# Attention with routed experts: rows of pages and of h turned by DMA transposes instead of TensorE

## The chip, the cores and the metric

The kernel runs on one core of a Trainium2 chip. The metric is the device time of one execution in microseconds, lower is better. Three runs of the kernel before gave 420.01, 420.77 and 420.65 us, median 420.65. The profile was taken in an execution of its own, which took 408.61 us.

## What is computed

The reference is block-causal attention over 8 sequences with 8 heads, 576 positions and head width 64, followed by a layer of 8 experts, of which each of the 4608 tokens uses one.

```python
scores = scale * np.matmul(q, k.transpose(0, 1, 3, 2))
mask = (pos[:, None] // 64) >= (pos[None, :] // 64)
attn = softmax(np.where(mask, scores, -1e9))          # written out in the reference
x = np.matmul(attn, v).transpose(0, 2, 1, 3).reshape(4608, 512)
logits = x @ w_gate                                   # 512 -> 8
expert_idx = np.argmax(logits, axis=1)
gate_w = softmax(logits)[np.arange(N), expert_idx]
for e in range(8):                                    # the rows of expert e
    h = np.maximum(x_sorted[lo:hi] @ w1[e], 0.0)      # 512 -> 1024
    y_sorted[lo:hi] = h @ w2[e]                       # 1024 -> 512
out = gate_w[:, None] * y
```

The softmax lines stand for the reference's own longer form; the rest is cut from it.

## The kernel before

**Attention.** The 64 (batch, head) slices are taken as 32 pairs of two heads; four pairs make one batch. The loop at L595 is a software pipeline written out by hand: the order of the instructions on TensorE, ScalarE and GpSimd is the order of the code, while VectorE's and SyncE's are placed by the compiler's priorities. In the turn of pair p, SyncE issues the loads of pair p+3 (q and k) and p+2 (v), GpSimd casts q and k of p+2 to f16 (`cast`, L202 and L204), TensorE computes the scores of p+1, the attention product of p (`attend`, L276), and the transposes of q and k of p+2 (`trans`, L212). `sums` adds the exponentials over key blocks on VectorE (L251, L257, L259). `denominators` (L282) then collects, in one PSUM tile, the softmax denominators (lhsT `picks`) and the router's logits (lhsT `wg`) as rows; VectorE copies it to `dl` (L305). `finish(p-1)` (L307) transposes the output of the pair before (L319, L322) and its `dl`, takes the reciprocals, and writes the scaled rows as f16 into `x16` and the scaled logits into `lgp`.

**Routing.** `choose` (L355) sums the logits of a batch and makes the one-hot choice `oh`. `route` (L376) counts with six small matmuls (L381, L385) how many earlier tokens of the batch chose the same expert. `places` (L392) turns the ranks into slots. `scatter` (L441, L447) sends the rows of the batch, 258 words each (512 f16 values in 256 words, then the gate weight and the number of the token), from GpSimd to the DRAM tile `xsorted`. That tile is made of pages of 128 rows, and each page belongs to one expert. The first ten pages are those known to be closed before the last two batches (`order1`); the others are listed in `order2`, which is written in the expert stage.

**Weights.** `load_weights(n)` (L125) is one of 32 DMAs on GpSimd's queue that read f32 and write f16 into `wall`. A partition p holds rows that lie next to each other in the matrix: `(p a b) f`. One such DMA is issued in each pair from the fourth on, two in each of the last three.

**Experts.** Each page is a tile T. `mload(T)` (L674) loads its 128 rows of 258 words with one SyncE DMA; the page's number comes from a register that SyncE loads from `order1` or `order2` (L670). `mtx` (L684) transposes the 512 columns in four TensorE transposes into PSUM, taking every fourth column to suit the weights' layout, and VectorE copies them to `xsT` (L691). `m1` (L698) is the first product, eight matmuls of 512 columns; ScalarE applies the relu (L708). `mth` (L711) transposes h in eight TensorE transposes, every eighth column, and VectorE copies (L718). `m2` (L721) is the second product, eight matmuls; ScalarE scales by the gate weight (L728) and GpSimd scatters the rows to the output by their token numbers (L729). `step(T)` (L737) issues m1(T), mtx(T+1), mth(T-1), m2(T-2), and loads page T+5. The last batch's finish and choice are in step 0, its ranks and scatters in step 1, `order2` in step 3. In this run 38 pages are in use.

In this stage only TensorE and ScalarE follow the code's order; SyncE does nothing but load pages, from ten buffers.

Of the kernel before, what the change touches and what calls it, by code (L numbers as in the profile page):

```python
# [10 lines left out]
I32 = mybir.dt.int32  # L11
# [11 lines left out]
def kernel(  # L23
# [33 lines left out]
    picks = consts.tile([128, 2, 32], F32)  # L57
    wg = consts.tile([128, HP, 32], F32)
    ione = consts.tile([128, E], F32)
# [22 lines left out]
    def gate_weights():  # L82
        nc.vector.memset(wg, 0.0)
        nc.vector.memset(picks, 0.0)
        for h in range(2):
            nc.vector.memset(picks[:, h, h:h + 1], 1.0)
        gate = moe_w_gate.rearrange("(hp h d) e -> h d hp e", h=2, d=64)
        for h in range(2):
            nc.sync.dma_start(out=wg[h * 64:h * 64 + 64, :, 8 + h * E:8 + h * E + E],
                              in_=gate[h])  # L90

# [33 lines left out]
    def load_weights(n):  # L125
        part, e, a = n // (2 * E), n // 2 % E, n % 2
        src = (moe_w1, moe_w2)[part][e].rearrange("(p a b) f -> p a (b f)", a=2, b=(2, 4)[part])
        nc.gpsimd.dma_start(
            out=wall[:, e, 8 * part + 4 * a:8 * part + 4 * a + 4, :].rearrange("p b f -> p (b f)"),
            in_=src[:, a, :])  # L130

    with tc.tile_pool(name="ld", bufs=2) as ld, \
# [14 lines left out]
        dls = [op.tile([128, 256], F32, name=f"dl{i}") for i in range(2)]  # L147
# [10 lines left out]
        def borders():  # L158
# [6 lines left out]
            for t in dls:  # L165
                nc.gpsimd.memset(t[:, 192:256], 1.0)
# [115 lines left out]
        def denominators(p):  # L282
# [5 lines left out]
            def add(t, cols, lhsT, src, start=False):  # L288
                nc.tensor.matmul(out=ps[32 * t:32 * t + 32, cols], lhsT=lhsT, rhs=src,  # L289
                                 start=start, stop=True, skip_group_check=True)  # L290
            lo, hi = slice(0, 128), slice(128, 192)
            for h in range(2):
                for j in range(4):
                    add(j, lo, picks[:, h, :],
                        acc[:, h, j * 128 - 128:j * 128] if j else pt[:, h, 0:128], h == 0)
            for h in range(2):
                add(h, hi, picks[:, h, :], acc[:, h, 384:448])
            for h in range(2):
                add(h, hi, picks[:, h, :], p4[:, h, :])
            for j in range(4):  # L300
                add(j, lo, wg[:, hp, :], oT[:, j * 128:j * 128 + 128])
            for t in (2, 3):
                add(t, hi, wg[:, hp, :], oT[:, 512:576])
            with tc.high_priority():
                st["dl"] = nc.vector.tensor_copy(dl[:, 0:192], ps)  # L305

        def finish(p, held=None):  # L307
# [3 lines left out]
            if hp == 0:  # L311
# [3 lines left out]
                st["lg", b] = op.tile([128, 5, H, E], F32, name="lgp")  # L315
# [5 lines left out]
            for n, src in enumerate((oT[:, 512:640], dl[:, 0:128], dl[:, 128:256])):  # L321
# [3 lines left out]
            nc.vector.reciprocal(rec[:, 4, :], ps2[:, 256:290:33])  # L325
            x16 = st["x16", b].bitcast(F16)
            for j, n, rows, logits in ((0, 4, ps, by_j[:, :, 8:24]),
                                       (4, 1, ps2[:, 0:128], ps2[:, 328:344].unsqueeze(1))):
                r = rec[:, j:j + n, :].unsqueeze(3)
                nc.vector.tensor_tensor(  # L330
                    out=x16[:, j:j + n, hp * 128:hp * 128 + 128].rearrange(
                        "p i (h d) -> p i h d", h=2),
                    in0=rows.rearrange("p (i h d) -> p i h d", h=2, d=64),
                    in1=r.to_broadcast([128, n, 2, 64]), op=ALU.mult)
                nc.vector.tensor_tensor(
                    out=st["lg", b][:, j:j + n, 2 * hp:2 * hp + 2, :],
                    in0=logits.rearrange("p i (h e) -> p i h e", h=2),
                    in1=r.to_broadcast([128, n, 2, E]), op=ALU.mult)

        def psum_small(i=1):  # L340
            return yps[i] if yps else t_ps.tile([128, 512], F32, name="tp")
# [13 lines left out]
        def choose(b):  # L355
            lg = rp.tile([128, 5, E], F32, name="lg")
            nc.vector.reduce_sum(out=lg, in_=st.pop(("lg", b)).rearrange("p j h e -> p j e h"),
# [18 lines left out]
        def route(b):  # L376
# [3 lines left out]
            rk_ps = psum_small()[:, 0:6 * E]  # L380
# [3 lines left out]
            for s in range(1, 6):  # L384
                nc.tensor.matmul(out=rk_ps[:, s * E:6 * E], lhsT=ones16,  # L385
                                 rhs=oh[:, 0:6 - s, :].rearrange("p j e -> p (j e)"),
                                 start=False, stop=(s == 5), skip_group_check=True)
            rk = rp.tile([128, 6, E], F32, name="rk")
            nc.scalar.copy(rk.rearrange("p j e -> p (j e)"), rk_ps)
# [166 lines left out]
        def last_order():  # L556
# [3 lines left out]
            ps = psum_small(0)[0:1, 0:2 * n]  # L560
# [6 lines left out]
        with tc.manual_schedule(engines={ET.PE, ET.Activation, ET.Pool}):  # L567
# [27 lines left out]
            for p in range(PAIRS):  # L595
# [12 lines left out]
                if p > HP and p % HP == 2:  # L608
                    places(p // HP - 1)
# [8 lines left out]
                if p > 2:  # L618
                    first = p - 3 + max(0, p - PAIRS + 3)
                    for n in range(first, first + 1 + (p >= PAIRS - 3)):  # L620
# [10 lines left out]
                if p > HP and p % HP == 1:  # L631
                    route(p // HP - 1)
                if p == PAIRS - 5:
                    first_places()
                if p == PAIRS - 4:
                    orders()
                denominators(p)
# [6 lines left out]
                if p >= HP and p % HP == 0:  # L644
                    with tc.high_priority():
                        choose(p // HP - 1)
                if p == PAIRS - 6:
# [6 lines left out]
            for e in range(E):  # L654
# [6 lines left out]
        xps = o_ps.tile([128, 512], F16, name="o0")  # L661
        hTps = o_ps.tile([128, F], F16, name="o1")
        xTs, hs, hTs, ys = ([m_sb.tile([128, w], dt, name=f"{n}{i}") for i in range(2)]
                            for n, w, dt in (("xsT", 512, F16), ("h16", F, F16), ("hT", F, F16),
                                             ("y", Dm, F32)))
# [8 lines left out]
        def mload(T):  # L674
            xs = xsp.tile([128, ROW], I32, name="xs")
            page = number(T, 0, ET.SP, NP - 1)
            ins = nc.sync.dma_start(
                out=xs, in_=xs_pages[:, ds(page, 1), :].rearrange("p a r -> p (a r)"))
# [143 lines left out]
```

## Time and profile before

| What | Value |
|---|---|
| median of three runs | 420.65 us |
| the profiled execution's own time | 408.61 us |
| its span, first to last instruction | 406.8 us |
| TensorE busy | 377.9 us, 93% |
| VectorE / ScalarE / GpSimd busy | 220.0 / 231.2 / 204.0 us |
| end of attention on TensorE | about 231.5 us |
| first product of tile 0, of tile 37 | 235.58 us, 391.12 us |
| end of the last second product | about 399.2 us |
| issue of the last scatter | 401.79 us |

A page of the profile gives the busy time of each engine, the span cut in 40 slices of 10.2 us with the busy share of each engine in tenths, the DMA queues, the chain of work that ended last, and the costliest groups of instructions. A line of a group or of the timeline names the engine, the line of the code, the operation, and the tiles it writes and reads. Matmuls overlap, so their durations can't be added: the distance from one start to the next is what counts. In lists of waits the columns are the waiting engine and line, what it waited for, the sum in us, the number of times and the longest. PE is TensorE, PEld its weight loads, DVE VectorE, ACT ScalarE, POOL GpSimd and SP SyncE; SPq is SyncE's queue of instructions, with the ones that issue DMAs.

### The profile page before, as it was taken

The numbers are of one execution on the slowest core, as the hardware profiler recorded it, in microseconds if no ns is written. First come the engines' busy times: TensorE is split into PE (matmuls) and PEld (weight loads), VectorE is DVE, ScalarE is ACT, GpSimd is POOL, SyncE is SP. The second block draws the span as 40 slices with busy tenths as digits, with TensorE's granted clock in tenths as the row PEclk, the third lists the DMA queues.
The fourth block names the chain that finished last, engine by engine and source line by source line (L and its number), as shares of the span: only waits on it lengthen the run. The fifth ranks groups of instructions, "written<-read, shape, count | busy, mean of one in ns | idle before, by whom it ended". The sixth has DMA issues, their size and how long they took to land.

```text
span 406.8 us, 11668 instructions
## 1 busy us (share of the span) xinstructions
PE 377.9 (93%) x4122; PEld 241.4 (59%) x4122; DVE 220.0 (54%) x683; ACT 231.2 (57%) x409; POOL 204.0 (50%) x430
## 2 busy tenths in 40 slices
PE   7899999899899899998998789999999999999992
PEld 6666667567576666675675555555555555555550
DVE  2546685886878876958978655222323222232320
ACT  4877767678677778676677223434444443434441
POOL 3666548569569477586494766412222121212222
PEclk9999999999999999999999989999999999999997
DMA  6798989999999999989998991332322222222212
GB/s 168 219 238 218 235 192 200 227 231 224 232 230 203 245 223 217 237 194 250 225 198 163 198 220 65 126 104 91 106 78 92 80 97 99 92 104 79 96 67 79
DMA packets 83068, 67.58 MB, mean 166 GB/s; under 512 B 52079, under 2 KB 75375, under 8 KB 83008
## 3 DMA queue, kind: packets, MB, share of 16 engines
q0 software_dynamic: 9824, 31.31, 33.9%
q1 hardware_dynamic: 72352, 34.89, 32.6%
q8 instruction: 37, 0.61, 0.6%
q10 hardware_dynamic: 832, 0.59, 0.5%
q14 instruction: 23, 0.19, 0.1%
HBM read 67.56 MB, written 17.23 MB: 208 GB/s over the span
## 4 chain that ended last, share of the span: by engine, by line
issue 26%; PE 25%; DMA 16%; POOL 16%; DVE 12%; ACT 2%; POOLq 1%; SPq 0%; ACTq 0%; DVEq 0%
PE o L276 9%; POOL out_dram L729 8%; PE tp L289 5%; DMA out_dram<-y,xs 4%; PE s L242 3%; DMA tl<-in_k_dram 3%; POOL xsorted L447 3%; POOL qk L202 2%; DMA qk<-in_k_dram 2%; PE o L212 2%; PE tp L319 2%; DMA xs<-xsorted 2%; POOL qk L204 2%; DMA xsorted<-x,slot 2%; PE tp L322 2%
## 5 line engine op out<-in xcount | busy, mean ns | idle before, releaser
L245 ACT ACTIVATE pt<-s 128x1024 f32<-128x1024 f32 x96 | 94.9, 1025 | 28.4 <-ACT qkT L217 10.9
L729 POOL DMA_INDIRECT out_dram<-y,xs x38 | 37.4, 984 | 110.8 <-ACT y L728 107.9
L276 PE MATMUL o<-pt,v 128*64 128x320 f32 (+3 forms) x768 | 90.0, 383 | 0.0
L703 PE MATMUL s<-wall,xsT 128*128 x304 | 73.1, 384 | 1.6 <-DVE xsT L691 1.1
L725 PE MATMUL tp<-wall,hT 128*128 x304 | 71.6, 379 | 0.0
L276 PEld LDWEIGHTS o<-pt,v 128*64 128x64 f32 x768 | 50.1, 137 | 35.4 <-issue 5.9
L691 DVE COPY xsT<-o 128x512 f16<-128x512 f16 x38 | 16.1, 423 | 100.9 <-PE o L687 100.9
L708 ACT ACTIVATE h<-s 128x1024 f16<-128x1024 f32 x38 | 38.9, 1023 | 50.3 <-PE s L703 50.3
L728 ACT ACTIVATE y<-tp,xs 128x512 f32<-128x512 f32 x38 | 26.1, 687 | 53.6 <-PE tp L725 53.6
L703 PEld LDWEIGHTS <-xsT 128*128 128x128 f16 x304 | 30.1, 99 | 37.9 <-issue 2.2
L447 POOL DMA_INDIRECT xsorted<-x,slot x40 | 43.4, 1085 | 10.1 <-issue 7.4
L247 POOL MEMSET pt<- 64x128 f32 x128 | 22.8, 200 | 46.2 <-ACT pt L245 34.8
L202 POOL CAST qk<-qk 128x512 f16<-128x512 f32 x62 | 41.1, 690 | 9.5 <-DMA qk<-in_q_dram 6.8
L725 PEld LDWEIGHTS <-hT 128*128 128x128 f16 x304 | 28.4, 98 | 27.1
L280 ACT COPY oT<-o 128x256 f32<-128x256 f32 x64 | 25.8, 403 | 29.3 <-PE o L276 29.3
L215 ACT COPY qkT<-o 128x512 f16<-128x512 f16 x62 | 36.9, 595 | 2.8 <-PE o L212 2.1
L251 DVE TENSOR_TENSOR acc<-pt 128x896 f32<-128x896 f32 x32 | 35.7, 1116 | 2.3 <-POOL pt L247 2.2
L305 DVE COPY dl<-tp 128x192 f32<-128x192 f32 x32 | 11.4, 355 | 47.1 <-PE tp L289 47.0
L257 DVE TENSOR_TENSOR acc<-acc,pt 128x640 f32<-128x640 f32 x32 | 35.2, 1099 | 0.1
L242 PE MATMUL s<-qkT 64*128 64x512 f16 (+4 forms) x320 | 32.0, 295 | 2.4 <-ACT qkT L215 1.3
L330 DVE TENSOR_TENSOR x<-tp,rec 128x512 f16<-128x512 f32 x64 | 31.1, 486 | 0.1
L718 DVE COPY hT<-o 128x1024 f16<-128x1024 f16 x38 | 26.3, 691 | 7.2 <-PE o L715 4.8
(153 smaller groups left out, 553.9 us busy)
## 6 DMA issues: line engine op xcount, KB each, us to landing
wall<-in_moe_w_dram POOLq DMA_DIRECT2D x32, 512.0 KB, 7.6
qk<-in_q_dram SPq DMA_DIRECT2D x32, 256.0 KB
v<-in_v_dram SPq DMA_DIRECT2D x64, 128.0 KB
qk<-in_k_dram SPq DMA_DIRECT2D x30, 256.0 KB
xs<-xsorted SPq DMA_DIRECT2D x43, 129.0 KB
xsorted<-fill SPq DMA_DIRECT2D x1, 1419.0 KB
tl<-in_q_dram SPq DMA_DIRECT2D x32, 32.0 KB
v<-in_v_dram SPq DMA_DIRECT2D x32, 32.0 KB
```

What stands on the lines that cost most here:

```text
L202: eng.tensor_copy(h16[:, n, 0:4].rearrange("p c h d -> p h c d"), qk[:, n].rearrange("p h (c d) -> p h c d", c=4))
L215: copy(qkT[:, n, 0:512].rearrange("d (p c) -> d p c", c=4), ps[:, 0:512].rearrange("d (c p) -> d p c", c=4))
L242: nc.tensor.matmul(out=sp[:, h, o:o + w], lhsT=qkT[r, 1, c * 128:c * 128 + 128], rhs=qkT[r, 0, q0:q0 + w], start=True, stop=True)
L245: nc.scalar.activation(pt[:, :, t * 512:t * 512 + 512], sp, AF.Exp, scale=scale)
L251: ins = nc.vector.tensor_tensor(out=acc[:, :, 0:448], in0=pt[:, :, 128:576], in1=pt[:, :, 576:1024], op=ALU.add)
L257: nc.vector.tensor_tensor(out=acc[:, :, 128:448], in0=acc[:, :, 128:448], in1=pt[:, :, 1024:1344], op=ALU.add)
L276: nc.tensor.matmul(out=o[h * 64:h * 64 + 64, q0 - lo:hi - lo], lhsT=vt[:, c, h, :], rhs=src, start=(c == 0), stop=(c == last), skip_group_ ...
L447: ins = nc.gpsimd.indirect_dma_start(out=xsorted[:, :], out_offset=bass.IndirectOffsetOnAxis(ap=slot[0:m, j:j + 1], axis=0), in_=x16[0:m, ...
L703: nc.tensor.matmul(out=hp[:, half * 512:half * 512 + 512], lhsT=xT[:, c * 128:c * 128 + 128], rhs=weight(T, 2 * c + half), start=(c == 0), ...
L708: nc.scalar.activation(h, hp, AF.Relu)
L725: nc.tensor.matmul(out=yp, lhsT=hT[:, f * 128:f * 128 + 128], rhs=weight(T, 8 + f), start=(f == 0), stop=(f == 7))
L729: ins = nc.gpsimd.indirect_dma_start(out=out[:, :], out_offset=bass.IndirectOffsetOnAxis(ap=xs[:, 257:258], axis=0), in_=y, in_offset=None ...
```

## The change

1. **Pages and h by DMA.** `mload` becomes two DMAs on SyncE: a DMA transpose of the page's 512 f16 columns straight into `xT`, and a small load of the last two words of each row, `gt`. `mtx` goes; the register of the page's expert is loaded by `expert(T)`. `mth` becomes one DMA transpose on SyncE from h into one of three `hT` buffers. It stands right behind m1(T). SyncE is now in the code's order too.
2. **Weights with rows 128 c + p.** The DMA transposes put column 128 c + p on partition p, so the weights' rows are loaded in that order: `(a b p) f`. A partition's share of one DMA is no longer one run but two (w1) or four (w2).
3. **Denominators' tile.** The last 64 positions' denominators and logits move into free rows of the same 128 columns, by lhsT `ones3` shifted and a second copy of the gate weights, `wg4`. So `dl` has 128 columns for 192 and `finish` transposes it once instead of twice.
4. **Ranks in the same tile.** `route` is split: `ranks` writes its six matmuls into columns 128 to 175 of the denominators' tile, behind them; `ranks_out` copies them on VectorE instead of ScalarE.
5. **Order.** `places` moves behind `finish`; `first_places` and `orders` go one pair later; weight loads 26 to 29 move up to pairs 28 and 29, none is left in pair 30 and two in pair 31. In the expert stage the last batch's ranks go from step 1 to 2, `last_order` from 3 to 4.

```diff
@@ gate_weights, load_weights @@
+            nc.sync.dma_start(out=wg4[h * 64:h * 64 + 64, :, h, 24:32], in_=gate[h])
...
-        src = (moe_w1, moe_w2)[part][e].rearrange("(p a b) f -> p a (b f)", a=2, b=(2, 4)[part])
+        b = (2, 4)[part]
+        src = (moe_w1, moe_w2)[part][e].rearrange("(a b p) f -> p a b f", a=2, b=b)
@@ denominators @@
             for h in range(2):
-                add(h, hi, picks[:, h, :], acc[:, h, 384:448])
+                add(h, 64, ones_at(2 + h), acc[:, h, 384:448])
...
-            for t in (2, 3):
-                add(t, hi, wg[:, hp, :], oT[:, 512:576])
+            for h in range(2):
+                add(2 + h, 64, wg4[:, hp, h, :], oT[:, 512:576])
+            if b is not None:
+                ranks(b, ps[:, 128:128 + 6 * E])
             with tc.high_priority():
-                st["dl"] = nc.vector.tensor_copy(dl[:, 0:192], ps)
+                st["dl"] = nc.vector.tensor_copy(dl, ps[:, 0:128])
+                if b is not None:
+                    ranks_out(b)
@@ finish @@
-            for n, src in enumerate((oT[:, 512:640], dl[:, 0:128], dl[:, 128:256])):
+            for n, src in enumerate((oT[:, 512:640], dl)):
@@ ranks_out, was in route @@
-            nc.scalar.copy(rk.rearrange("p j e -> p (j e)"), rk_ps)
+            nc.vector.tensor_copy(rk.rearrange("p j e -> p (j e)"), rk_ps)
@@ the loop over pairs @@
-                    first = p - 3 + max(0, p - PAIRS + 3)
-                    for n in range(first, first + 1 + (p >= PAIRS - 3)):
+                    until = {PAIRS - 4: 4 * E - 5, PAIRS - 3: 4 * E - 2, PAIRS - 2: 4 * E - 2,
+                             PAIRS - 1: 4 * E}
+                    for n in range(until.get(p - 1, p - 3), until.get(p, p - 2)):
                         load_weights(n)
...
-                denominators(p)
+                denominators(p, p // HP - 1 if p > HP and p % HP == 1 else None)
@@ mload, was one load of all 258 words @@
+            xT = xsp.tile([128, 4, 128], F16, name="xT")
+            gt = xsp.tile([128, 2], I32, name="gt")
             page = number(T, 0, ET.SP, NP - 1)
+            rows = xs_pages[:, ds(page, 1), :].rearrange("p a r -> p (a r)")
+            for ins in (nc.sync.dma_start_transpose(out=xT, in_=rows.bitcast(F16)[:, 0:512]),
+                        nc.sync.dma_start(out=gt, in_=rows[:, 256:258])):
@@ mth @@
-            for f in range(8):
-                nc.tensor.transpose(ps[:, f * 128:f * 128 + 128],
-                                    h[:, f:F:8], ident16)
-            hT = hTs[T % 2]
-            nc.vector.tensor_copy(hT, ps)
+            hT = hTs[T % 3]
+            nc.sync.dma_start_transpose(out=hT.rearrange("p (c t) -> p c t", t=128),
+                                        in_=pg.pop(("h", T)))
@@ step @@
             if T < n:
                 m1(T)
+                mth(T)
+            if T + 1 < n:
+                expert(T + 1)
...
-            if T + 1 < n:
-                mtx(T + 1)
-            if 0 <= T - 1 < n:
-                mth(T - 1)
             if 0 <= T - 2 < n:
                 m2(T - 2)
@@ order of the last stage @@
-        with tc.manual_schedule(engines={ET.PE, ET.Activation}):
+        with tc.manual_schedule(engines={ET.PE, ET.Activation, ET.SP}):
```

## The prediction

> **What bounds it now.** I read the page's slices first, then the chain of waits, the timeline of one expert tile, the waits on TensorE, and SyncE's own instructions. The slices show two stages:
>
> ```profile
> PE   7899999899899899998998789999999999999992
> DMA  6798989999999999989998991332322222222212
> ...
> q0 software_dynamic: 9824, 31.31, 33.9%
> q1 hardware_dynamic: 72352, 34.89, 32.6%
> ```
>
> TensorE is full in both. The DMA engines are full up to slice 23 (attention, with the weight loads beside it) and a quarter busy after (experts). The chain names "issue" and the out scatter L729 for the expert stage, because it follows the last scatter back along GpSimd; that engine idles 3 us of every tile. The timeline shows what really paces it:
>
> ```profile
> 299.77 1.46 PE L703 MATMUL s<-wall,xsT 128*128 x6
> 301.07 0.39 PE L687 MATMUL o<-ident,xs 128*128 128x128 f16 x4
> 301.29 0.66 PE L715 MATMUL o<-ident,h 128*128 128x128 f16 x8
> 301.33 1.02 ACT L708 ACTIVATE h<-s 128x1024 f16<-128x1024 f32 x1 [1.05 <-PE s L703]
> 301.79 1.89 PE L725 MATMUL tp<-wall,hT 128*128 x8
> 303.51 1.89 PE L703 MATMUL s<-wall,xsT 128*128 x8
> 304.72 0.98 POOL L729 DMA_INDIRECT out_dram<-y,xs  x1 [3.18 <-ACT y L728]
> 305.24 0.39 PE L687 MATMUL o<-ident,xs 128*128 128x128 f16 x4
> ```
>
> Read start to start, as matmuls overlap: second product 301.79 to 303.51 = 1.72 us, first product 303.51 to 305.24 = 1.73, twelve transposes 301.07 to 301.79 = 0.72. The tile's period is 4.17, no gap in it: TensorE alone is the bound. In attention a plain pair takes 6.49 us (denominators start 91.73, 98.22), also TensorE without gaps; four pairs of one batch take 27.88 (78.11 to 105.99), 1.9 more than 4 x 6.49. The waits on TensorE, 50 to 218 us, say where most of it sits:
>
> ```profile
> PE tp L381 <- DVE oh L372: 5.3, 6, 0.9
> PE tp L319 <- DVE dl L305: 3.0, 6, 0.5
> PE tp L322 <- DVE dl L305: 1.6, 5, 0.9
> ```
>
> The rank matmuls stand ahead of the denominators and wait 0.9 us a batch for the one-hot choice; then VectorE is late with dl.
>
> **What the Trainium skill says.** (1) "DMA: Bandwidth & Descriptors", Anatomy of one DMA: about 2.0 us fixed plus bytes over 436 GB/s. For the 256 KB scatter that is 2.6 us; the trace's median is 2.8 from issue to landing, so it agrees. (2) Same page, Latency and other measured facts: a DMA transpose moved 261 GB/s with a non-contiguous middle dimension, 350 to 400 contiguous. No run here shows one. (3) "VectorE: DVE Perf Modes", The three transpose paths: 128x128 in bf16 is 390 ns on TensorE and 1309 ns by DMA. Here TensorE takes 0.72/12 = 0.06 us each back to back, so that table is latency, not pace; whether the DMA figure is too is the question of this case. (4) The first page, Specifications: runs of 512 B or more go at line rate.
>
> **Part by part.** The sum is against the profiled execution: span 406.8, its own time 408.61; the median of the runs is 420.65, 12.04 above, which I carry over unchanged.
>
> Expert tile. Removed: 12 transposes, 0.72 us of TensorE, and the two VectorE copies L691 (0.42) and L718 (0.69), which hide beside it. Left: 1.72 + 1.73 = 3.45. Tiles 5 to 37 run at the steady pace (first products at 257.62 and 391.12, 32 periods). The DMA engines must then hold: rows 128 KB + h 256 KB turned, 384 KB at 261 GB/s = 1.5 us, plus what the period has now, 0.28 x 4.17 = 1.2 us (the row load in it goes): 2.7 of 3.45. The 128 pieces of 8 bytes of gt are small: 29 ns each (q1: 32.6% of 16 x 406.8 us over 72352 packets), 0.23 us over 16 engines. So the period fits, with 0.5 to spare.
>
> Latency of hT. From the start of m1(T) h is ready at 1.73 + 0.25 + 1.02 = 3.0 us; m2(T) is two and a half periods on, 8.6. The turn has 5.6 us to be seen. Estimate from (1) and (2): 2.0 + 256 KB/261 GB/s = 3.0, plus SyncE's issue. Three hT buffers keep it from waiting for m2.
>
> SyncE. Its queue is now in program order: turn of h(T), then page number, turn of rows and gt of T+5. From the trace:
>
> ```profile
> L670 SPq TENSOR_LOAD <-order x43: 262/271/732, 211.1 to 383.9; - x43
> L677 SPq DMA_DIRECT2D xs<-xsorted x43: 332/333/466, 225.4 to 386.9; - x43
> ```
>
> 0.27 + 0.33 + 0.33 = 0.93 us plus the turn of h. That issue isn't shown: from 0.33 (as a plain load) to the 0.60 of a qkv load, or several times that if it is issued in blocks. I take 1.0; it begins to pace at 3.45 - 0.93 = 2.5. I book a period of 3.48: 32 x (4.17 - 3.48) = **-22**.
>
> Behind the waiting turn stand the page loads. Two places hurt. At step 5 the load of page 10 waits for the last batch's scatters (issued to 254.6 now, seen by SyncE at 257.8); ranks move from step 1 to 2, about 1 us later against m1(0); h(6) is then some 0.7 us late, covered by the 5.6. At step 34 seven page loads of about 1.1 us stand between the turns of h(34) and h(35): 7.7 us where h(35) comes 3.5 after h(34). The turn is 4 to 5 late, slack is about 1.5: **+4**, and +1 for step 5's neighbourhood. Before, SyncE served nobody else and this was free.
>
> First tiles (235.58 to 257.62, 22.0 us for five): the same 0.7 a tile goes, part of it into waits for pages and ScalarE: **-2**. Tail: m1(37) to m2(37) is 6.2 us now (391.12, 397.28); with h ready at 3.0, a turn of 4 to 4.5 gives 7 to 7.5: **+1.5**; the last scatter after it is unchanged.
>
> Attention. (a) One f32 transpose of dl less in each finish: 0.16 us (L322: 99.99 to 100.30 is two), x 28 pairs = -4.5, if TensorE stays the bound. (b) Ranks behind the denominators: the 1.04 us of denominator matmuls cover the 0.92 wait, 7 batches: -6.3; the L319 wait (0.5) goes with the ranks' own buffer, but ps2 now waits for two VectorE copies, dl (0.36, narrower now) and rk (0.22): about -0.2 net, -1.5. places behind finish: the last use of slot is the scatter one pair later, covered. (c) Against it, GpSimd and DMA. The weights' pieces shrink from one run of 8 KB a partition to 4 KB (w1) and 2 KB (w2), above 512 B, so line rate by (4); but GpSimd writes 256 and 512 pieces for 128. Its issue is 0.588 us now; bounds +0 and four times for w2, +1.8. The casts end at 103.70 for TensorE's transposes at 104.05: 0.35 us of cover, in the two pairs of a batch that scatter. And the iota L313 waits for a scatter that lands 7.7 us later (156.01); its cast has 2.3 us of cover, of which (b) takes 1.4. I give back half of the 12: **-7** (from -12 to +3). gate_weights' extra memset and two 8 KB loads stand at the start on VectorE and SyncE, under the first loads: 0 to +0.7, taken as 0.
>
> Start of the experts. TensorE waits 2.3 us for the first page, then 0.54 for its transposes and 0.42 for their copy; loads 27 to 29 go ahead of pair 30, away from the page loads: **-2** (from -5 to +2).
>
> Sum: -22 + 5 - 2 + 1.5 - 7 - 2 = -26.5; profile 408.61 to 382, runs 420.65 to **394**.
>
> **Rivals.** *DMA paces in part* (turns of 3.7 to 4.2 us a tile, as latency or as traffic): for it, the 256-byte pieces of a turn and h's two-buffer loop (relu of T+2 waits for the turn of T); against it, the three-quarters idle DMA in this stage. At 3.95: 32 x 0.22 = -7 instead of -22, so 409. *Slower: the one turn queue paces the tiles.* Price: 1309 ns a block by (3) less the 0.68 us that the DMA page's measured bandwidth table has for any small transfer = 0.63 us for 32 KB, 12 blocks = 7.6 us a tile. 36 x (7.6 - 4.17) = +123; with the other terms (-4.5): 539. It decides from 4.17 + 4.5/32 = 4.3 us a tile, that is 384 KB at 91 GB/s. For it: turns are serial on one queue and the next rows' turn waits behind h; against: the page's 261. A mild form, 4.3 to 5, ends at 421 to 443. *Attention eats its gain* (GpSimd's piece writing, full DMA engines): +3 for -7, so 404.
>
> **Chances.** Forecast, 385 to 403: 0.50. Attention without gain, and DMA in part, 403 to 421: 0.23. Queue paces mildly, to 445: 0.09; fully, about 540: 0.18. The range 382 to 445 holds the first three, 0.82. A measurement of this kernel can tell 0.2% (0.8 us): faster 0.71, same 0.02 (the upper end of the second case), slower 0.27.
>
> **What would show it.** Right: TensorE period 3.45 to 3.5 with no L687/L715 rows; the turns landing under 5 us; one gap near step 35; no wait of L381 in attention, batches of 26 to 27 us; the weights' issue on GpSimd under 0.8. Wrong: second products waiting on hT in every tile (queue), SyncE's issue above 2.5 us, or casts late each batch.

## The result and the profile after

Four runs of the changed kernel took 441.39 to 446.62 us, median 443.68, beside 420.71 for the kernel before in the same comparison: ratio 1.055 (95% interval 1.048 to 1.062), slower by 5.5%. The forecast was 394, so it had the wrong sign. The time lies at the upper end of the range, in the case to which the prediction gave 0.09 ("Queue paces mildly, to 445"). Ratios here and below are taken over the runs within 1.5% of a kernel's fastest, medians over all of its runs; where the two tell different things (e10 and e13) both are given.

The profiled execution took 446.62 us, span 444.6. Its slices and queues, to be laid beside those of before:

```profile
PE   7889999989899899797998677786988788988260
PEclk9999999999999899999999969999999998999767
DMA  6798998999989989999899948976766768676341
...
q1 hardware_dynamic: 136416, 44.88, 47.5%
q0 software_dynamic: 18016, 31.31, 35.5%
```

A slice is 11.1 us now. In the expert stage (the last 16 digits or so) TensorE, which had 9 almost everywhere, shows mostly 6 to 8, and the DMA engines went from 2 or 3 to 6 or 7. The turns do cost DMA time, with nearly twice the packets on q1, but the engines aren't full. TensorE's second product names what it waits for, in the list of the costliest groups (behind the bars: busy us, mean ns, idle before it and its releaser):

```profile
L723 PE MATMUL tp<-wall,hT 128*128 x304 | 76.6, 399 | 40.6 <-DMA hT<-h 37.2
```

Before, no wait of this kind existed. The 37.2 us alone are more than the whole transposes were worth (38 x 0.72 = 27 us). That names the transfer, but not what made it late: the turn itself, the DMA engines, or the engine that issues it. SyncE's timeline tells, since between its rows stand only small register work and the load of the page's number, which this view leaves out:

```profile
346.29 1.28 SPq L715 DMA_TRANSPOSE hT<-h  x1
348.56 1.24 SPq L687 DMA_TRANSPOSE xT<-xsorted  x1
350.06 0.36 SPq L688 DMA_DIRECT2D gt<-xsorted  x1
350.52 1.25 SPq L715 DMA_TRANSPOSE hT<-h  x1
```

From 346.29 to 350.52 is one tile, 4.23 us, and the next ones begin at 354.69, 358.83 and 363.01. In the tile SyncE issues 1.28 + 1.24 + 0.36 = 2.88 us of DMAs; between 347.57 and 348.56 it loads the page's number (L677, 0.81 us here); register work and gaps make up the last 0.5. It doesn't wait in it. **SyncE's issue takes 4.2 us a tile, which by chance is what TensorE took before (4.17).**

How far SyncE lags behind, ScalarE's rows show. By the order of relus and turns, the turn at 346.29 belongs to the relu at 340.11, and the relu at 349.51 waits until that turn has read the same buffer:

```profile
340.11 1.02 ACT L710 ACTIVATE h<-s 128x1024 f16<-128x1024 f32 x1 [1.10 <-DMA hT<-h]
349.51 1.02 ACT L710 ACTIVATE h<-s 128x1024 f16<-128x1024 f32 x1 [2.17 <-DMA hT<-h]
```

So h was ready at 341.13 and stood 5.2 us in SyncE's queue, while the turn itself, from the start of its issue, took 3.2.

Two places come on top. At step 34 seven pages are loaded between two turns of h, and TensorE stands:

```profile
405.58 1.23 SPq L687 DMA_TRANSPOSE xT<-xsorted  x1
407.02 0.42 SPq L688 DMA_DIRECT2D gt<-xsorted  x1
407.89 1.20 SPq L687 DMA_TRANSPOSE xT<-xsorted  x1
...
421.57 0.35 SPq L688 DMA_DIRECT2D gt<-xsorted  x1
422.59 5.61 SPq L715 DMA_TRANSPOSE hT<-h  x3
425.91 1.02 ACT L710 ACTIVATE h<-s 128x1024 f16<-128x1024 f32 x1 [12.84 <-DMA hT<-h]
425.95 1.44 PE L723 MATMUL tp<-wall,hT 128*128 x3 [11.93 <-DMA hT<-h]
```

A page costs 2.3 us of SyncE (405.58 to 407.89), not the 1.1 of the forecast. The second place is attention. The waits on TensorE from 50 to 218 us, in the form of those of before:

```profile
PE tp L332 <- DVE dl L314: 12.4, 10, 2.4
```

The wait for the one-hot choice (L381 before, 5.3 us) is gone as forecast; the wait for `dl`, 4.6 us before, is 12.4 and single ones reach 2.4. By stretches of the two spans, 406.8 and 444.6 (relu n is the start of the relu of tile n, on ScalarE):

| Stretch | Before, us | After, us | Difference | The forecast's terms |
|---|---|---|---|---|
| start to relu 0 (attention, first page) | 238.8 | 247.0 | +8.2 | -7 and -2 |
| relu 0 to 4 | 16.6 | 22.1 | +5.5 | -2 and +1 |
| relu 4 to 35 | 129.3 | 136.0 | +6.7 | -22 |
| relu 35 to 37 (seven page loads) | 8.4 | 20.8 | +12.4 | +4 |
| relu 37 to the end | 13.7 | 18.7 | +5.0 | +1.5 |
| sum | 406.8 | 444.6 | +37.8 | -26.5 |

The table overstates the loss against the runs (+23.0): the profile of before took 408.61 where its runs took 420.71, that of after 446.62 among runs of 441 to 447. The 12 us that the prediction carried over from profile to runs did not carry over. The kernel before takes 407 to 408 us on one chip used here and 421 on others. On the first of these its profile looks like the one before the change (spans of 404.4 and 406.8 us in e9 and e17 below), so the 12 us were most likely the difference between two chips, and a part of the table's differences can be the chip's too. Each experiment below is compared only with the kernel before on its own chip.

### The profile page after: what moved, and what is told of

The parts are those of the page before. It is cut to its first block, busy times and chain, and to the rows that moved or that the text cites. A ratio compares the mean times of both kernels' runs of the same rounds, so it can differ in the third digit from the quotient of the medians.

```text
span 444.6 us, 10726 instructions
## 1 busy us (share of the span) xinstructions
PE 366.1 (82%) x3634; PEld 215.9 (49%) x3634; DVE 179.6 (40%) x615; ACT 230.7 (52%) x401; POOL 212.2 (48%) x429
## 5 line engine op out<-in xcount | busy, mean ns | idle before, releaser
L723 PE MATMUL tp<-wall,hT 128*128 x304 | 76.6, 399 | 40.6 <-DMA hT<-h 37.2
L727 POOL DMA_INDIRECT out_dram<-y,gt x38 | 37.4, 983 | 131.1 <-ACT y L726 130.0
L281 PE MATMUL o<-pt,v 128*64 128x320 f32 (+3 forms) x768 | 94.0, 396 | 0.0
L705 PE MATMUL s<-wall,xT 128*128 x304 | 73.5, 386 | 2.1 <-DMA xT<-xsorted 1.8
L457 POOL DMA_INDIRECT xsorted<-x,slot x40 | 48.4, 1211 | 13.4 <-issue 7.3
L726 ACT ACTIVATE y<-tp,gt 128x512 f32<-128x512 f32 x38 | 26.2, 688 | 51.5 <-PE tp L723 41.2
L705 PEld LDWEIGHTS <-xT 128*128 128x128 f16 x304 | 30.3, 100 | 40.0 <-issue 3.8
L314 DVE COPY dl<-tp 128x128 f32<-128x128 f32 x32 | 9.2, 289 | 53.2 <-PE tp L294 50.6
L217 PE MATMUL o<-ident,qk 128*128 128x128 f16 x320 | 24.3, 223 | 2.2 <-POOL qk L207 2.2
L209 POOL CAST qk<-tl 64x256 f16<-64x256 f32 x32 | 25.4, 792 | 0.5 <-DMA tl<-in_k_dram 0.3
```

Of the source, the lines that this page charges most:

```text
L281: nc.tensor.matmul(out=o[h * 64:h * 64 + 64, q0 - lo:hi - lo], lhsT=vt[:, c, h, :], rhs=src, start=(c == 0), stop=(c == last), skip_group_ ...
L457: ins = nc.gpsimd.indirect_dma_start(out=xsorted[:, :], out_offset=bass.IndirectOffsetOnAxis(ap=slot[0:m, j:j + 1], axis=0), in_=x16[0:m, ...
L705: nc.tensor.matmul(out=hp[:, half * 512:half * 512 + 512], lhsT=xT[:, c, :], rhs=weight(T, 2 * c + half), start=(c == 0), stop=(c == 3))
L723: nc.tensor.matmul(out=yp, lhsT=hT[:, f * 128:f * 128 + 128], rhs=weight(T, 8 + f), start=(f == 0), stop=(f == 7))
L727: ins = nc.gpsimd.indirect_dma_start(out=out[:, :], out_offset=bass.IndirectOffsetOnAxis(ap=gt[:, 1:2], axis=0), in_=y, in_offset=None, bo ...
```

## The experiments

The theory of this document: the expert stage is paced by what SyncE has to issue for each tile. Its rivals were that the turns are paced by the DMA engines or by their latency, and that the loss sits in attention, with the weights' smaller pieces as the cause or `places` in its new position.

### Parts of the change alone

`e1_attn_only`: the changed attention and weights, the expert stage of before with TensorE's transposes. `e2_moe_only`: the attention of before, the weights and the expert stage of after. `e3_weights_only`: the kernel before with the new weights; TensorE's transposes then take contiguous columns.

```diff
-                                    h[:, f:F:8], ident16)
+                                    h[:, f * 128:f * 128 + 128], ident16)
```

> The changed kernel's attention (weights with rows 128 c + p, one dl transpose, ranks in the denominators' tile, the new order) with pages and h turned on TensorE as before. Theory 1 (VectorE's own chain from the choice to the slots now paces two pairs of each batch; the expert stage's loss is SyncE's): batches of 29 us instead of 27.9, the experts start 7 to 10 us later, total +6 to +10 against before, expert tiles 4.17 us. Rival (the loss in attention comes only with the turns or from a lowered TensorE clock): total within 2 us of before.

> Before's attention (its denominators, route, order of places), with the weights in rows 128 c + p and the new weight schedule, and the changed kernel's expert stage. Theory 1: SyncE issues 1.25 (h) + 1.20 (rows) + 0.36 (gt) + 0.27 (page number) us and the time between them, 4.2 us a tile, so no gain in the steady stage, and the seven page loads at the end cost 12 us: total +12 to +18, expert tiles 4.2 us. Rival (traffic of the turns on the DMA engines): the same period, but with SyncE's queue waiting rather than issuing. If attention were innocent, the whole +23.

> The kernel before, with nothing changed but the weights' rows (128 c + p; two or four pieces a partition for one) and the contiguous columns in TensorE's transposes that go with it. Theory 1: the issue on GpSimd goes from 0.59 to 0.8 us and hides, total 0 to +2. Rival (smaller pieces fill the DMA engines, which makes attention late): +6 to +10.

Measured, all on one chip beside 407.23: e1 414.96, ratio 1.021 (1.013 to 1.029); e2 429.65, 1.052 (1.046 to 1.058); e3 409.16, 1.005 (1.003 to 1.007). So most of the loss is the expert stage, the weights by themselves are nearly free, and the changed attention loses where it was to gain 7. In e2, attention's batches keep 27.9 us, tiles average 4.27, relu 35 to 37 is longer by 12 us and the tail by 4.3. One cost goes with the weights in every kernel here: from the issue of the last scatter to the end it takes 8.0 us with the new rows and 4.7 to 5.3 with the old. Why isn't known.

### What paces a tile

`e4_h_by_dma` was to have h alone turned by DMA, rows by TensorE:

```diff
-            for f in range(8):
-                nc.tensor.transpose(ps[:, f * 128:f * 128 + 128],
-                                    h[:, f:F:8], ident16)
-            nc.vector.tensor_copy(hT, ps)
+            nc.sync.dma_start_transpose(out=hT.rearrange("p (c t) -> p c t", t=128),
+                                        in_=pg.pop(("h", T)))
```

> Before's attention with the new weights' rows; only h is turned by DMA (two buffers, behind m1), pages are loaded whole and turned on TensorE; of the pages past 36 two are loaded ahead and the others where they are found in use. Theory 1: SyncE issues about 1.25 + 0.33 + 0.27 us and gaps, 2.5 us a tile, so TensorE paces at 3.45 + 0.23 = 3.7 us: total -12 to -16. Rival (a turn of h takes 8 us from h to landing whatever SyncE does): m2 waits for hT in each tile, period 4.2 or more, total 0 or slower.

Measured: 627.78 us beside 407.23, ratio 1.542. The kernel held a slip of mine. With two `hT` buffers and the turn of h(T) ahead of m2(T-2), the second product multiplies the turn just issued, that of a tile two later: it uses the wrong h, and every tile waits for a whole turn. So it tells nothing on the theory, but it measures the latency, from the start of the issue to the first matmul that uses it:

```profile
308.68 1.26 SPq L715 DMA_TRANSPOSE hT<-h  x1
312.29 1.69 PE L723 MATMUL tp<-wall,hT 128*128 x5 [4.52 <-DMA hT<-h]
```

3.61 us, of which 1.26 are issue. The forecast had 3.0 plus issue within a slack of 5.6, and in the changed kernel the turn above took 3.2, so the latency of a turn alone doesn't make h late.

`e5_two_pages_ahead` is the changed kernel with the seven page loads of step 34 spread: two there, the others one by one when the page is due. `e6_gt_on_scalar` is e5 with the small load of the gate words on ScalarE's queue; ScalarE loads the page's number for it by itself.

```diff
-                for t in range(ends[0], NP):
+                for t in range(ends[0], ends[1]):
                     mload(t)
...
+                for t in range(ends[level + 1], (ends + [NP])[level + 2]):
+                    mload(t)
```

```diff
-            page = number(T, 0, ET.SP, NP - 1)
-            rows = xs_pages[:, ds(page, 1), :].rearrange("p a r -> p (a r)")
+            rows, tail = (xs_pages[:, ds(number(T, 0, e, NP - 1), 1), :].rearrange(
+                "p a r -> p (a r)") for e in (ET.SP, ET.Activation))
...
-                        nc.sync.dma_start(out=gt, in_=rows[:, 256:258])):
+                        nc.scalar.dma_start(out=gt, in_=tail[:, 256:258])):
```

> The changed kernel with one edit: in step 34 SyncE loads two of the seven pages past 36, the next ones stand in the branch that finds them in use. Theory 1: the 16 us in which SyncE turned seven pages between h(34)... and the last h go to about 5 (twice 2.3), so 10 to 12 us come back: against before +11 to +13 instead of +23. Rival (the end is late for another reason, the turns' landing): within 3 us of the changed kernel.

> As the run with two pages ahead, and the small load gt is issued on ScalarE's queue, which loads the page number for itself; SyncE keeps both turns, the bytes moved are the same. Theory 1 (SyncE's own instructions pace: 1.26 h, 0.81 page number, 1.22 rows, 0.36 gt and the time between them are 4.2 us without a wait): 0.55 to 0.6 us a tile less, period 3.6, so about 15 to 18 us less than the run with two pages ahead; against before -3 to -6. Rival (the DMA engines or the landing of the turns pace): period stays at 4.2, no difference.

Measured on one chip beside 420.91: e5 435.02, 1.032 (1.027 to 1.037); e6 416.46, 0.983 (0.979 to 0.987). Relu 35 to 37 fell from 20.8 to 13.0 us in e5; its tiles still mostly take 4.1 to 4.4. e6 moves the same bytes by the same turns, and only takes 0.36 us and the register work around it off SyncE. Four of its relus:

```profile
301.31 1.02 ACT L710 ACTIVATE h<-s 128x1024 f16<-128x1024 f32 x1 [1.04 <-issue]
304.76 1.02 ACT L710 ACTIVATE h<-s 128x1024 f16<-128x1024 f32 x1 [1.04 <-PE s L705]
308.22 1.02 ACT L710 ACTIVATE h<-s 128x1024 f16<-128x1024 f32 x1 [1.04 <-issue]
311.67 1.02 ACT L710 ACTIVATE h<-s 128x1024 f16<-128x1024 f32 x1 [1.04 <-PE s L705]
```

They come every 3.45 us, TensorE's two products and nothing else, and where these rows name a releaser it is TensorE. From relu 4 to 35 the median tile takes 3.45 us (4.21 in e5) and the mean 3.80 (4.41), since some relus still wait for a turn, 6.0 us in all (26.0 in e5). This decides against both rivals: the DMA engines and the latency allow 3.45. 18.6 us over some 33 tiles is 0.56 us a tile, for one 1 KB load.

`e7_h_by_dma` repeats e4 without the slip: attention of before, the new weights, three buffers for `hT` (the third in place of `acc`), page loads spread as in e5. Rows stay on TensorE; SyncE has one turn and one plain load a tile.

```diff
+        hTs.append(acc.rearrange("p h w -> p (h w)").bitcast(F16)[:, 0:F])
...
-            hT = hTs[T % 2]
+            hT = hTs[T % 3]
```

> Before's attention with the weights' new rows; h turned by DMA into three buffers (the third lies where acc was), behind m1; pages loaded whole and turned on TensorE; two pages ahead as above. Theory 1: SyncE has 1.26 + 0.81 + 0.35 us and little between, 2.6 a tile, the turn of h lands 3.6 us after its issue (as seen with two buffers), less than the 5.5 there are: TensorE paces at 3.45 + 0.24 = 3.7 us. Against before -10 to -14. Rival (the turn's landing paces): m2 waits for hT in each tile, 4 us or more.

Measured beside 420.91: 412.66, ratio 0.981 (0.977 to 0.985). It is the lowest ratio of all, though e6, e8 and e15 (0.983 each) lie within its interval. TensorE's rows:

```profile
302.13 1.89 PE L724 MATMUL tp<-wall,acc 128*128 x8
303.86 1.89 PE L706 MATMUL s<-wall,xsT 128*128 x8
305.59 0.39 PE L690 MATMUL o<-ident,xs 128*128 128x128 f16 x4
305.81 1.89 PE L724 MATMUL tp<-wall,hT 128*128 x8
```

1.73 + 1.73 + 0.22 = 3.68 us, no wait in it: eight of the twelve transposes are saved in full, and the turn is hidden. Relu 4 to 35 takes 112.9 us; in e8, on the same chip with the expert stage of before, it takes 127.4. The change's idea works where SyncE has room.

### Attention

`e8_denominators_only`: changed attention, old weights, old expert stage. `e9_before_again` is the kernel before, for scale. `e10_places_back` is e8 with `places` in its old position, for the rival that `places` behind `finish` delays VectorE:

```diff
                 sums(p)
+                if p > HP and p % HP == 2:
+                    places(p // HP - 1)
...
                 finish(p - 1)
-                if p > HP and p % HP == 2:
-                    places(p // HP - 1)
```

> The kernel before with the changed attention alone: one dl transpose, ranks in the denominators' tile, rk copied on VectorE, places behind finish, first_places and orders a pair later; the weights and the expert stage are before's. Theory 1 (VectorE's chain from the choice to the slots, and the dl copy behind it): +5 to +7. Rival (the weights' pieces are needed for the loss): within 2 us of before.

> The kernel before, unchanged, for its profile on this chip. Both theories: ratio 1.00 within its interval. If the profile again takes some 10 us less than the timed runs, the attention parts of profiles are compared only with each other.

> The changed attention alone (old weights, old expert stage), with places back in its old position ahead of the scores of its pair. Theory 1 (places stands ahead of the next dl copy on VectorE, and TensorE waits for that): if the position matters, the waits of L332 for dl fall from about 7 us (50 to 218 us) to under 4, and the time by 2 to 4 us against the run with the denominators only. Rival (VectorE orders by readiness, the work itself is the bound): the same waits, no difference.

Measured: e8 412.49 beside 420.91, 0.983 (0.976 to 0.989); e9 407.80 beside 408.33, 0.998 (0.997 to 1.000); e10 407.31 beside 408.33, 0.992 (0.989 to 0.995) or 0.998 by the medians, batches of 27.1 us. With the old weights the changed attention gains. Its wait for `dl`:

```profile
PE tp L330 <- DVE dl L312: 6.1, 6, 1.8
```

6.1 us in e10, 7.2 in e8 and 12.7 in e1. With the old weights the place of `places` matters little: e12, below, has it behind `finish` on the chip of e10, and its batches take 27.3 us, its wait 7.5. To part `places` from the weights, `e13_attn_places_back` is e1 with `places` back, beside `e14_denominators_again`, which repeats e8, and `e15_h_and_places_back`, which is e13 with e7's expert stage.

> The changed attention with the new weights' rows, on before's expert stage (as the first run), with places back ahead of the scores of its pair. Theory 2 (places behind finish puts 4.5 us of VectorE work right before the next dl copy; with the small weight pieces beside it the two add up): back to within 3 us of before, the waits of L332 for dl under 7 us. Rival (the small pieces alone): still +6 to +9.

> The changed attention with the old weights, places behind finish, once more, beside the others on one chip. Theory 2: slower than the run with places back by 2 to 4 us, about equal to before. Rival (position of no matter): equal to places back, -3 against before.

> New weights' rows, changed attention with places back, h turned by DMA into three buffers, pages turned on TensorE, two pages ahead. Theory 1 and 2: tiles of 3.68 us as with h by DMA, attention no slower than before's: -10 to -14 against before. Rival (the small pieces cost the attention its gain): as h by DMA alone, -7 to -9.

Measured on one chip beside 421.33: e13 0.995 (0.992 to 0.998), but its median of 424.18 is 1.007 of that of before, so neither a gain nor a loss is shown. e14 414.76, 0.987 (0.982 to 0.992); e15 414.47, 0.983 (0.977 to 0.990), tiles of 3.68. In e13 the wait stays:

```profile
PE tp L332 <- DVE dl L314: 12.7, 10, 2.8
```

So the position of `places` doesn't make this wait, a theory of mine that fell; it comes with the new weights, together with the changed attention. e1 and e13 ran on different chips, so their times can't settle whether the position adds a little with the new weights. `e17_before_third` and `e18_attn_again` repeat the kernel before and e1.

> The kernel before, unchanged. If the chip is one on which it takes 421 us, its profile shows where those 13 us are against 408: in the attention's batches (28.5 us and more instead of 27.9) or as halved TensorE clock. Otherwise 1.00 and the same profile as before.

> The changed attention with the new weights' rows on before's expert stage once more, beside a profile of before. Theory 2 (places behind finish and the small pieces add up): +5 to +9 against before, and slower than the run with places back. Rival (the place is of no matter, the small pieces with the changed attention are the loss): as the run with places back, whose waits for dl were 12.7 us as here.

Measured beside 407.75: e17 407.95, 0.999 (0.996 to 1.002); e18 417.79, 1.026 (1.017 to 1.034). On this chip the parts alone are 0.992 (e10) and 1.005 (e3), together 1.021 and 1.026, where 0.992 x 1.005 is 0.997: 10 to 12 us come from their meeting, or 7 to 9 by the medians. The batches say the same: on average 27.1 us in e10 and 28.4 in e3, against 27.9 before, but 29.4 in e1 and 29.1 in e18. It isn't a single cost.

The trace suggests how, in the changed kernel around 113 us (argued from the order of the rows, not shown by a run of its own). GpSimd's issue of one DMA of weights is 0.79 us, 0.59 before, and the write of `x16` and GpSimd's iota wait for the scatter of the batch before to land:

```profile
113.08 0.69 DVE L341 TENSOR_TENSOR x<-tp,rec 128x512 f16<-128x512 f32 x1 [0.85 <-DMA xsorted<-x,slot]
113.09 0.13 POOL L324 IOTA x<- 128x5 int32 x1 [3.00 <-DMA xsorted<-x,slot]
...
119.22 0.17 DVE L433 CAST slot<-sl 128x5 int32<-128x5 f32 x1
119.30 0.28 DVE L314 COPY dl<-tp 128x128 f32<-128x128 f32 x1
119.63 0.33 PE L332 MATMUL tp<-ident,oT 128*128 128x128 f32 x1 [1.94 <-DVE dl L314]
```

VectorE's arithmetic of the slots (114.95 to 119.39) follows late, and the copy of `dl` behind it; TensorE waits 1.94 us. The wait of the `x16` write is what differs between the kernels. From 50 to 218 us, on one chip, first e18 with the new weights, then e10 with the old:

```profile
DVE x L341 <- DMA xsorted<-x,slot: 3.6, 4, 1.3
DVE x L339 <- DMA xsorted<-x,slot: 1.2, 2, 0.7
```

e1 has 4.2 and e12 1.1. The wait of the iota is there in all of them, 6.9 to 9.2 us, and 5.5 in the kernel before. Why it grows with the new weights isn't shown. After the wait of 1.94 us TensorE runs slow, as the view by stretches says (after the stretch and its length: busy us and instructions of TensorE, its weight loads, VectorE, ScalarE and GpSimd, then granted clock, DMA share and GB/s):

```profile
114.00:117.00 3.00, 3.00 (x66) 2.34 (x62) 2.93 (x15) 2.16 (x6) 2.73 (x8) 1.00 1.14 282
120.50:124.00 3.50, 3.50 (x20) 1.90 (x20) 2.60 (x9) 2.19 (x3) 1.49 (x4) 0.51 1.08 269
```

Clock 1.00 before the wait, 0.51 after it. The attention product behind took 4.48 us instead of 2.81, so a wait of 1.94 cost 1.7 more here. It isn't so after each wait: of the six of 1.9 to 2.4 us in this kernel's attention, four had the half clock behind them, while those that end at 90.5 and 180.0 (1.95 and 2.09 us) were followed by 3.5 us at 1.00. The Trainium skill, "TensorE: Matmul & The Clock Gate", Part 1: The HAM clock gate, says that an idle window of about 3.4 us puts the array at half its clock and a busy one of that length frees it again. The 0.51 over 3.5 us agrees with the second; for the first, waits of 1.94 to 2.4 us were enough in four cases of six.

### Keeping the old weights

If the weights could stay, the turn by DMA would need h's columns in another order. Three kernels try it: `e11_h_in_relu_order` lets the relu write them so; `e12_h_relu_denominators` is e11 with the changed attention; `e16_h_in_matmul_order` takes the first product's moving columns in steps of eight.

```diff
-            nc.scalar.activation(h, hp, AF.Relu)
+            nc.scalar.activation(h.rearrange("t (f p) -> t p f", f=8),
+                                 hp.rearrange("t (p f) -> t p f", f=8), AF.Relu)
```

```diff
+        def wide_row(T, c):
+            return wall[:, ds(pg["e", T], 1), 2 * c:2 * c + 2, :].rearrange(
+                "p a b (q f) -> p f (a b q)", f=8)
...
-                                     rhs=weight(T, 2 * c + half),
+                                     rhs=wide_row(T, c)[:, half * 4:half * 4 + 4, :],
```

> The kernel before with old weights' rows (one run of 8 KB a partition), old attention; only h is turned by DMA, behind m1, into three buffers; ScalarE's relu writes h in the order in which the turn gives every eighth column to a partition, so the weights need no new rows; two pages ahead. Theory 1: as the run with h by DMA, but without the weights' cost in attention: tiles of 3.7 us, -14 to -17 against before. Rival (the strided write makes the relu slower than 1.02 us, h comes late and the turn paces): 4 us a tile or more.

> As the run with h in relu order, and the changed attention (one dl transpose, ranks in the denominators' tile, places behind finish) with the old weights. Theory 1 (that attention loses by VectorE's chain): 3 to 7 us slower than h in relu order alone. Rival (without the small weight pieces it loses nothing): within 3 us of it, or faster.

> Old weights' rows, changed attention with places back, h turned by DMA; the first product takes its moving columns with a step of eight, so h comes out in the order that the turn needs. Theory 1: if TensorE reads the stepped columns at its usual pace, tiles of 3.7 us and -16 to -20 against before. Rival (stepped columns slow the eight matmuls of the first product, as the strided write slowed the relu): tiles of 4.5 us and more, slower than before.

Measured: e11 457.00 beside 408.33, 1.121 (1.116 to 1.126); e12 451.05, 1.104 (1.098 to 1.110); e16 640.41 beside 421.33, 1.523 (1.516 to 1.530). All three miss by far. In e11 one line gives the cause, min/median/max in ns:

```profile
L708 ACT ACTIVATE h<-s x38: 4702/4776/5057, 239.3 to 435.6; 128x1024 f16<-128x1024 f32 x38
```

4.78 us for 1.02: ScalarE became the bound. In e16 it is TensorE, 7.36 for 1.89:

```profile
401.53 7.36 PE L713 MATMUL s<-wall,xsT 128*128 x8
```

The Trainium skill, "SBUF — State Buffer", Door 1: The DMA port swizzle, notes lines of 16 bytes, each new one at a price. Steps of 256 bytes (relu's output) and 16 bytes (moving columns) leave a line at every element, and the two durations fit that. The price isn't the same everywhere: h in steps of 16 bytes, loaded as the weights of TensorE's transposes, took 0.146 us a load in the kernel before and 0.098 without steps (e3). e12 against e11 is a side result: 6 us less, so the changed attention gains with the old weights here too.

## Why the prediction was wrong

**The step that failed is SyncE's sum**: "0.27 + 0.33 + 0.33 = 0.93 us plus the turn of h", 1.0, with pacing from 2.5 on. By terms, in the tile shown: the turn of h, 1.0, measured 1.28, within its bounds; the turn of the rows, priced as the plain load that it replaced, 0.33, measured 1.24; the page's number, 0.27, measured 0.81, where it now stands behind a turn; gt, 0.33, measured 0.36; register work and gaps, not counted, 0.54. Together 4.23 for 1.93. The paragraph gave h's turn a range up to several times a plain load and then used the load's price for the other turn. With 1.2 in both places and the rest as it was, the sum is about 3.0, still below 3.45; the 0.54 more of the number and the 0.54 of the gaps took it over. One of these was there to see: the line of L670, quoted in the prediction, has a maximum of 0.73.

**Expert tile, -22.** TensorE's 3.45 was right: the median tile of e6 shows it, e7 shows 3.68 with the rows' transposes. The DMA engines had room, as worked out. The gain existed and SyncE took it: +6.7 in place of -22, which is 28.7 of the 64.3 us between the forecast (-26.5) and the profile (+37.8).

**Rival "the one turn queue paces the tiles".** Its mild form is what happened, at 4.2 to 4.4 us a tile, but not by its mechanism. It priced a block's turn at 0.63 us, 7.6 a tile; e6 turns the same blocks in 3.45. The queue is paced by its issue, which depends on what else stands in it.

**The seven page loads, +4.** Place and mechanism right, size wrong: pages of 2.3 us instead of 1.1, and 12.4 in place of 4. e5 gets 7.8 of it back.

**First tiles, -1, and tail, +1.5.** Relu 0 to 4 came out at +5.5. The page loads don't explain it, since the five ahead of the first tile end where the first turn of h begins. That turn is the slow one:

```profile
248.13 4.43 SPq L715 DMA_TRANSPOSE hT<-h  x1
258.00 3.57 PE L723 MATMUL tp<-wall,hT 128*128 x8 [4.48 <-DMA hT<-h]
```

Its issue took 4.43 us for 1.25, and 9.9 us passed from its start to the product that uses it; in e2, on the chip of 407 us, it was 4.28 and 10.1. Why isn't known. Of the tail's +5.0 the last turns account for 2.0; the other 3.0 come after the last scatter and go with the weights, as in e3.

**Latency.** 3.2 and 3.6 us measured, 4 to 4.5 supposed: the room was there, as worked out. The estimate rests on the Trainium skill, "DMA: Bandwidth & Descriptors": a fixed 2.0 us (Anatomy of one DMA, stated there for DMAs that GpSimd issues) and 261 GB/s (Latency and other measured facts). It gave 3.0, or 4.3 with the measured issue of 1.26; e4 has 3.61 with it, so it was somewhat high.

**Attention, -7.** The wait of L381 went as forecast, and with the old weights the gain is there: 6.6 and 8.4 us in e14 and e8, 1 to 3.3 in e10. (Half of the prediction's 12 is 6, not the 7 that it booked.) The term for the weights was a single bound on GpSimd's issue ("bounds +0 and four times for w2, +1.8"; measured 0.2) and passed over what they do together with `dl`: +8.2 up to the first relu instead of -9, of which e1, on the chip of 407 us, shows 4.7. The rival "attention eats its gain" (+3 for -7) had the right place and too small a price.

**Open.** The kernel before takes 407 or 421 us by chip. A part of it is seen: e7 has the attention code of e2, but batches of 28.8 us on its chip for 27.9, plain pairs of 6.8 to 7.1 for 6.49, with TensorE idle by up to 0.5 us where the trace names no releaser. That is 6 us over seven batches; no profile of the kernel before was taken on such a chip, and the cause wasn't found. Another part shows at the start of the experts: with the expert stage of before, relu 0 to 4 takes 23.3 us in e8 and 27.1 in e14, but 16.4 in e10 on the chip of 407. So e7's 0.981 holds against 420.91; its 412.66 is above the 407 of the kernel before on the other chip, where e7 was not run. A version with e6's relief for SyncE and attention of e10 was not tried: the turn needs the new weights.

## What to carry to other kernels

When work moves from a compute engine to DMAs, sum what the issuing engine does for each tile, register loads and gaps included, and give every DMA transpose the price of a transpose; compare that sum with the tile's period, whatever the bandwidth allows. A queue that issues DMA for a pipeline can't take a burst of other loads: spread them, or give small ones to another queue. A change of layout that looks free alone can cost where a wait for its DMA meets another engine's chain, so try it together with what it will stand beside.

## What the hardware showed that was not expected

- Issue of a DMA transpose on SyncE: 1.20 us for the 128 KB of rows from DRAM and 1.25 for the 256 KB of h, so hardly by size, beside 0.33 for a plain load.
- The load of a page's number into a register of SyncE took 0.27 us in the kernel before and 0.78 (median) behind DMA transposes. "DMA: Bandwidth & Descriptors", Latency and other measured facts, in the Trainium skill, gives `tensor_load` a floor of about 600 ns; the 0.27 is below it.
- After a wait of 1.94 us TensorE had half its clock (0.51) for the next 3.5 us; in the batch after, a wait of 2.2 us had an attention product of 4.50 us behind it again. Two other waits of about 2 us had no such effect.
- The first DMA transpose of h took 4.4 us to issue and was used 9.9 us after its start, the later ones 1.25 and 3.2.
- Columns in steps: a relu that writes 256 bytes apart took 4.78 us for 1.02; moving columns 16 bytes apart made eight matmuls 7.36 us for 1.89.
- TensorE's transposes of contiguous columns instead of every fourth or eighth took the median tile from 4.17 to 4.12 us (e3).
